# Two load queues, a full-width leftover pass, a third product buffer and new orders in a one-core FFT and MLP kernel

## The chip, the cores and the metric

The kernel runs on 1 core of one Trainium2 chip. The metric is the device time of one execution in microseconds (us), as the median of several runs. A profiled execution gives the trace that the text reads; its engines are called PE (matmul), PEld (weight load), DVE, ACT, POOL and SP, as in the profile.

## The reference

```python
def reference(A_x, A_w_r, A_w_i, B_x, B_w_gate, B_w_up, B_w_down):
    x = A_x                                   # (1, 2048, 576) bf16
    h = x + A(layernorm(x), A_w_r, A_w_i)     # A: rfft2 over both axes, times (w_r + i w_i), irfft2
    return h + B(layernorm(h), B_w_gate, B_w_up, B_w_down)
    # B(x) = (gelu(x @ w_gate) * (x @ w_up)) @ w_down, F = 4608
```

A is a two-dimensional real Fourier transform of the 2048 x 576 input, a product with a given spectrum and the transform back. B is a gated MLP. Each has a layer norm ahead of it, without scale and shift, and a residual.

## The kernel before

Everything is written engine by engine: a small class `Prog` records operations with the tiles that they read and write, puts each on the engine named, in the order in which it is recorded, and places the semaphore waits. Nothing is scheduled at run time. The order comes from three strings of short words that loops read: `SEQ1` (the front: first layer norm and first transform step), `SEQF` (the spectral middle) and `SEQ` (transform back, second layer norm, start of the MLP). A word is a letter for an operation and a number; a last letter A, D or P names the engine (ACT, DVE, POOL). Since each engine runs in order, a word's place counts only against the words of the same engine, and whatever waits holds up all that is behind it on its engine.

*Loads.* `LORD` lists the pieces of x (tile XO, 16 row tiles of 128 x 576) and of the cos/sin table (ATB, 16 tiles of 128 x 128) in order of issue; "x4-8" is tiles 4 to 7 of x. All are issued by SP, followed there by the other tables (FT, BT, VT, DT, ...) and the spectrum (WS).

*The front* (`SEQ1`). The 16 tiles form six groups, (0,2), (2,4), (4,7), (7,10), (10,13), (13,16). Three tiles (3, 4 and 13) get their statistics on ACT, a sum (`S`, L471) and a sum of squares (`Q`, L475); the others on DVE by two half-width `bn_stats` each (`B`, L480). Then for each group: `v` the variance (L486, L488, L491), `q` the square root on ACT (L495), `c` the reciprocal on DVE (L500), `x` the scaled table ATS = ATB times the reciprocal deviation (POOL L505, or DVE L510), `n` the negated right half of x into XN (POOL L552), `M` the matmuls (L536), `E` the copy of their result from PSUM into U (L547, on ACT or DVE). For the last groups `E` copies the first half of U's columns and `F` the second. `k` stands for dummy matmuls on a zero tile ZD (L521): k14 is 14 of them at the start, k104 four for group 1's bank, k202 two for group 2's.

In `M` five passes k = 0 to 4 go over the columns of x. Passes 0 to 3 add or subtract 128-column pieces of the left and right half. Pass 4 takes the leftover columns 256 to 287 and 544 to 575, as two matmuls with 32 output rows each:

```python
parts = [(XO[:, c, 256 + 288 * h:288 + 288 * h], 32 * h, 32 * h + 32, True, True) for h in range(2)]
```

so pass 4 fills 64 of 128 partitions of U, and POOL zeroes the others first (L466). PSUM has 8 banks and a group uses five in turn, so a group's matmuls also wait for older evictions.

*The middle* (`SEQF`), for 16 column groups: `D` six matmuls with FT on U (L606) and an ACT copy to CUS; `B` four matmuls with BT (L616) and an ACT copy to YS (L598); `T` products of YS with the spectrum into TP (DVE L625); `Z` sums of TP into ZS and ZR (DVE L636, L639); `V` four matmuls with VT (L646) and an ACT copy to V; `R` two matmuls for the last 32 columns (L658) and a masked copy into VR on DVE (L661); `w` the negated imaginary spectrum (DVE L630). TP, CUS and YS rotate through 2, 3 and 2 buffers.

*The start of the second half* (`SEQ`): `I` and `N` transform back (L731, L774), the residual add (L791) and the second layer norm for six row tiles (`s`, `q`, `c`, `n`, `e`), `z`, `D`, `A` transpose a normalised tile through PE (L836), and `g`, `h` are the first MLP matmuls. After that come the MLP's four blocks of gate/up matmuls (L872) and down matmuls (L973), with the other ten row tiles worked in between.

Of the kernel before, what the change touches and what calls it, by code (L numbers as in the profile page):

```python
# [4 lines left out]
BF16 = mybir.dt.bfloat16  # L5
F32 = mybir.dt.float32
ACTF = mybir.ActivationFunctionType
ALU = mybir.AluOpType

S, D, K2 = 2048, 576, 289  # L10
KW = 288
HK = 144
NZ = 5
# [10 lines left out]
SEQ1 = """k14 Q3 B1 B0 n0 S3 n2 v0 B2 v1 q0 q1 c0 x0D M0 S4 c1 Q4 B5 B6 E4A E2A v2 B7 q2 n1 E0A E1A x1P c2 k104 M1 B8 x2P B9 E6A n3 v3 E3A E5A E8A q3 k202 M2 B10 B12 E9A n4 E11A E12A S13 c3 B11 E10A E7A v4 x3P M3 B14 q4 c4 E13A E14A x4P B15 Q13 v5 E17A q5 E16A E15D M4 c5 E19A E20A x5D E18D E23A n5 E22D E21D E24A M5 E25A F23D F24A E26A F25D E27A E29A F29A E28D F28D F22A F26D F27A""".split()  # L24
LORD = "x0-2 x2-4 a0-4 x4-8 a4-8 x8-12 x12-16 a8-16".split()
SPLIT = tuple(int(w[1:-1]) for w in SEQ1 if w[0] == "F")
ACT_TILES = tuple(int(w[1:]) for w in SEQ1 if w[0] == "Q")
SEQF = """w0 w1 D0 D1 D2 B0 T0 D3 B1 Z0 T1 B2 D4 T2 D5 Z1 B3 B4 T3 D6 Z2 w2 D7 Z3 B5 V1 V0 T4 T5 Z4 B6 w3 B7 T6 D8 Z5 T7 V2 D9 Z6 B8 T8 V3 Z7 V4 D10 B9 R0 D11 V5 Z8 B10 T9 R1 T10 B11 D12 Z9 V6 D13 Z10 B12 T11 D14 T12 B13 V8 Z11 V7 B14 T13 Z12 D15 Z13 T14 V9 R2 V10 Z14 B15 V13 T15a T15b V11 Z15a V12 Z15b R3 V14 V15 R4""".split()
VENG = [('act',), ('act',), ('act',), ('act',), ('act',), ('act',), ('act',), ('act',), ('act',), ('act',), ('act',), ('act',), ('act',), ('act',), ('act',), ('act', 'act')]
DENG, BENG = ['act', 'act', 'act', 'act', 'act', 'act', 'act', 'act', 'act', 'act', 'act', 'act', 'act', 'act', 'act', 'act'], ['act', 'act', 'act', 'act', 'act', 'act', 'act', 'act', 'act', 'act', 'act', 'act', 'act', 'act', 'act', 'act']  # L30
SEQ = """I0 I1 N0 I2 s0 N1 I3 S1 q0 N2 I4 c0 e0 s2 q1 n0 n1 N3 I5 c1 z0 n2 s3 e1 D1 N4 N5 e2 q2 c2 n3 e3 D2 g10 g00 h10 z3 h00 g20 g01 h20 h01 g21 g11 h21 h11""".split()
# [14 lines left out]
def build_tables():  # L46
# [36 lines left out]
    def ang(d, k):  # L83
        return np.pi * (((2 * d[:, None] + 1) * k[None, :]) % (2 * D)) / D

    fr = np.zeros((6, 128, 2, HK))
    dr = np.concatenate([np.arange(256, 288), np.arange(544, 576)])
    for o, kk in enumerate((k2o, k2e)):
        for h, fn in enumerate((np.cos, np.sin)):
            for t in range(2):  # L90
                fr[3 * o + t, :, h] = fn(ang(np.arange(128 * t, 128 * t + 128), kk))
            fr[3 * o + 2, 0:64, h] = fn(ang(dr, kk))
# [220 lines left out]
def _build(nc, A_x, A_w_r, A_w_i, B_w_gate, B_w_up, B_w_down, out):  # L313
# [28 lines left out]
    XN = sb.alloc("XN", [128, NT, 288], BF16)  # L342
# [49 lines left out]
    TP = sb.alloc("TP", [128, 2, 2, 2, KW], BF16)  # L392
# [15 lines left out]
    def bank(b, p0=0, p1=128, c0=0, c1=512):  # L408
        return PS[p0:p1, b * 512 + c0:b * 512 + c1]
# [15 lines left out]
    def x_load(i, c0, c1):  # L425
        P.dma(SP, XO[:, c0:c1, 0:D], xv[:, c0:c1, :], f"x{i}", w=[("X", c) for c in range(c0, c1)])

    def atb_load(i, c0, c1):
        P.dma(SP, ATB[:, c0:c1, :], tabs[:, c0:c1, :], f"atb{i}", w=[("ATB", c) for c in range(c0, c1)])

    for i, w in enumerate(LORD):
        (x_load if w[0] == "x" else atb_load)(i, int(w[1:].split("-")[0]), int(w.split("-")[1]))
# [33 lines left out]
    P.op(POOL, lambda g: g.memset(U[64:128, 4, :, :, :], 0.0), w=["Uz"])  # L466
# [11 lines left out]
    def ln1_tile(c):  # L478
        for h in range(2):
            P.op(DVE, lambda v, c=c, h=h: v.bn_stats(ST1[:, c, h, :], XO[:, c, 288 * h:288 * h + 288]), r=[("X", c)], w=[("ST1", c, h)])  # L480

    def ln1_var(i):
        c0, c1 = GROUPS[i]
        for c in range(c0, c1):
            if c in ACT_TILES:
                P.op(DVE, lambda v, c=c: v.tensor_scalar(TM[:, 0, c:c + 1], SA[:, 0, c:c + 1], SA[:, 0, c:c + 1], 1.0 / (D * D), op0=ALU.mult, op1=ALU.mult), r=[("SA0", c)], w=[("TM", c)])  # L486
            else:
                P.op(DVE, lambda v, c=c: v.bn_aggr(MV1[:, c, :], ST1[:, c, :, :]), r=[("ST1", c, 0), ("ST1", c, 1)], w=[("MV1", c)])  # L488
        for c in range(c0, c1):
            if c in ACT_TILES:  # L490
                P.op(DVE, lambda v, c=c: v.tensor_scalar(MV1[:, c, 1:2], SA[:, 1, c:c + 1], 1.0 / D, TM[:, 0, c:c + 1], op0=ALU.mult, op1=ALU.subtract), r=[("SA1", c), ("TM", c)], w=[("MV1", c)])  # L491
# [23 lines left out]
    def a_bank(i, k):  # L515
        return (5 * i + AORD.index(k) + ABASE) % 8
# [6 lines left out]
    def a_mm(i):  # L523
        c0, c1 = GROUPS[i]
        for k in AORD:
            b = a_bank(i, k)
            for c in range(c0, c1):
                o = 128 * (c - c0)
                if k == 4:
                    parts = [(XO[:, c, 256 + 288 * h:288 + 288 * h], 32 * h, 32 * h + 32, True, True) for h in range(2)]  # L530
                else:
                    d0 = 128 * (k // 2)
                    x2 = XN[:, c, d0:d0 + 128] if k % 2 else XO[:, c, 288 + d0:416 + d0]
                    parts = [(XO[:, c, d0:d0 + 128], 0, 128, True, False), (x2, 0, 128, False, True)]
                for lhs, p0, p1, s, e in parts:
                    P.op(PE, lambda t, b=b, lhs=lhs, p0=p0, p1=p1, s=s, e=e, o=o, c=c: t.matmul(bank(b, p0, p1, o, o + 128), lhs, ATS[:, c, :], start=s, stop=e),  # L536
                         r=[("X", c), ("ATS", c)] + ([("XN", c)] if k % 2 else []), w=[("PS", b)])

    def a_ev(n, eng, late=False):
        i, k = n // 5, AORD[n % 5]  # L540
        hs = (1,) if late else (0,) if n in SPLIT else (0, 1)
        g0, g1 = 8 * hs[0], 8 * hs[-1] + 8
        c0, c1 = GROUPS[i]
        m, b, w = c1 - c0, a_bank(i, k), 64 if k == 4 else 128
        src = bank(b, 0, w, 0, 128 * m).rearrange("p (n g e) -> p n g e", n=m, g=16)[:, :, g0:g1, :]
        dst = U[0:w, k, g0:g1, c0:c1, :].rearrange("p g n e -> p n g e")
        fn = (lambda v: v.tensor_copy(dst, src)) if eng == DVE else (lambda a: a.activation(dst, src, ACTF.Copy))  # L547
        P.op(eng, fn, r=[("PS", b)] + ([("EV", n)] if late else []), w=[("U", i, k, h) for h in hs] + ([] if late else [("EV", n)]))

    def x_neg(i):  # L550
        c0, c1 = GROUPS[i]
        P.op(POOL, lambda g: g.tensor_scalar(XN[:, c0:c1, :], XO[:, c0:c1, 288:D], -1.0, 1.0, op0=ALU.mult, op1=ALU.mult),  # L552
             r=[("X", c) for c in range(c0, c1)], w=[("XN", c) for c in range(c0, c1)])

    ENG = {"A": ACT, "D": DVE, "P": POOL}
    RUN1 = {"k": idle_mm, "S": act_sum, "Q": act_sq, "B": ln1_tile, "v": ln1_var, "q": ln1_sqrt, "c": ln1_rs, "M": a_mm, "x": ln1_scale, "E": a_ev, "F": lambda n, eng: a_ev(n, eng, True), "n": x_neg}
    P.op(ACT, lambda a: a.activation(SA[:, 0, 0:1], EPT[:, 0:1], ACTF.Sqrt), r=["EPT"], w=[("SA0", 0)])
# [14 lines left out]
    P.alias([("XN", c) for c in range(NT)], [("V", g, c) for g in range(NG) for c in range(2)])  # L572
    uk = [[("U", i, k, h) for i in range(len(GROUPS)) for h in range(2)] + (["Uz"] if k == 4 else []) for k in range(5)]
# [27 lines left out]
    def st_D(i, eng=ACT):  # L601
        b0, s3 = FB["D", i], i % 3
        for o in range(2):
            b = b0 + o
            for m, us in enumerate((1 - o, 3 - o, 4) if o == 0 else (4, 1 - o, 3 - o)):
                P.op(PE, lambda t, b=b, m=m, us=us, o=o: t.matmul(bank(b, 0, 128, 0, 2 * HK), U[:, us, i, :, :], FT[:, 3 * o + (2 if us == 4 else us // 2), :], start=(m == 0), stop=(m == 2)),  # L606
                    r=[("U", q, us, i // 8) for q in range(len(GROUPS))] + (["Uz"] if us == 4 else []) + ["FT"], w=[("PS", b)])
        ev(eng, CUS[:, s3, :, :].rearrange("p a (j r) -> p a j r", r=2), banks(b0, 2, 2 * HK).rearrange("p r (a j) -> p a j r", a=2),
           [("PS", b0), ("PS", b0 + 1)], [("CU", s3)])
# [10 lines left out]
    def st_T(i, q0=0, q1=KW, hs=(0, 1)):  # L620
        g, sl = GORD[i], i % 2
        w3 = WS[:, 1, g, 1 + q0:1 + q1]
        w4 = bass.AP(w3.tensor, w3.offset, [list(w3.ap[0]), [NG * K2, 2], [-NG * K2, 2], [1, q1 - q0]])
        y4 = YS[:, sl, :, q0:q1].unsqueeze(1).to_broadcast([128, 2, 2, q1 - q0])
        P.op(DVE, lambda v: v.tensor_tensor(TP[:, sl, :, :, q0:q1], y4, w4, op=ALU.mult),  # L625
             r=[("Y", sl), ("Wn", i)] + (wkeys[0] if 1 <= g < 9 else wkeys[1] if g else wkeys[0] + wkeys[1]), w=[("T", sl, h) for h in hs])
# [6 lines left out]
    def st_Z(i, hs=(0, 1)):  # L633
        sl, z3 = i % 2, i % NZ
# [291 lines left out]
    P.alias([("ATB", c) for c in range(NT)], [("AT", f) for f in gu_early])  # L926
# [14 lines left out]
    fdead += [("T", a, h) for a in range(2) for h in range(2)] + [("Z", a) for a in range(NZ)] + [("ZR", a, h) for a in range(2) for h in range(4)]  # L941
# [102 lines left out]
```

## Time and profile before

| | us |
|---|---|
| median of 3 runs (lowest, highest) | 491.55 (491.47, 491.59) |
| profiled execution | 491.75 |
| its span, first to last instruction | 490.0 |
| PE busy in the span | 482.7 |
| first matmul of M0 | 7.29 |
| first matmul of stage D | 20.22 |
| first matmul of I0 | 48.66 |
| first MLP matmul (L872) | 57.40 |

The span is that of the slowest, here the only, core. Busy time of PE is the time in which at least one matmul is under way, with modelled ends. A row of a group of instructions gives busy time, the mean of one, and the idle time of its engine just before them with what ended it. The granted TensorE clock is 1.000 for the core. Idle time of an engine matters only where the chain of waits passes through it.

### The profile page before, as it was taken

To read this page: it belongs to the slowest core of one execution; us is meant where nothing else is said; L and a number is where in the kernel's file an instruction comes from. 1 tells how busy PE (TensorE), PEld (TensorE's weight loads), DVE (VectorE), ACT (ScalarE), POOL (GpSimd) and SP (SyncE) were. 2 spreads that over 40 slices of the span, in tenths; PEclk is the share of its full clock that TensorE was granted. 3 is DMA by queue.
4 is the path that set the end of the run, shared out by engine and by line. 5 is a ranking of instruction groups with operands and counts; after the bars stand their busy time and mean duration, and the time that the engine had idled before them with its cause. 6 is when DMAs were issued, how large, how long until landed. Compare 5 with 4: busy or idle time off the path is not lost.

```text
span 490.0 us, 9967 instructions
## 1 busy us (share of the span) xinstructions
PE 482.7 (99%) x4391; PEld 311.6 (64%) x4392; DVE 193.6 (40%) x397; ACT 151.2 (31%) x297; POOL 31.8 (6%) x58
## 2 busy tenths in 40 slices
PE   7999999999999999999999999999999999999998
PEld 3787788888888744444577644444677544444775
DVE  6799733433576634333311144433211233333111
ACT  6999743223322222322200033233100122323000
POOL 6411441000000020000000000000000000000000
DMA  8990999100001071100000001000000000000000
GB/s 284 248 313 6 354 363 351 30 15 2 1 16 37 18 233 23 26 1 1 2 18 16 17 18 23 17 1 0 7 19 19 7 1 0 1 2 1 13 20 18
DMA packets 25148, 31.20 MB, mean 64 GB/s; under 512 B 11440, under 2 KB 17840, under 8 KB 25104
## 3 DMA queue, kind: packets, MB, share of 16 engines
q1 hardware_dynamic: 22208, 18.62, 13.1%
q0 software_dynamic: 2896, 11.95, 7.0%
q8 instruction: 34, 0.56, 0.5%
q14 instruction: 10, 0.08, 0.1%
HBM read 26.22 MB, written 2.36 MB: 58 GB/s over the span
## 4 chain that ended last, share of the span: by engine, by line
PE 94%; DVE 2%; DMA 1%; issue 1%; POOL 0%; ACT 0%; SPq 0%; DVEq 0%; POOLq 0%
PE PS L872 57%; PE PS L973 29%; PE PS L606 2%; PE PS L536 2%; DMA XO<-in_A_x_dram 1%; PE PS L890 1%; PE PS L616 1%; PE PS L731 1%; DVE TP L625 1%; PE PS L774 1%; PE PS L646 1%; PE PS L908 1%; DVE VR L661 0%; DVE ZS L636 0%; POOL XN L552 0%
## 5 line engine op out<-in xcount | busy, mean ns | idle before, releaser
L872 PE MATMUL PS<-HT,WG 64*128 64x512 bf16 (+1 forms) x2160 | 229.0, 371 | 0.1
L872 PEld LDWEIGHTS PS<-HT,WG 64*128 64x128 bf16 x2160 | 130.3, 94 | 96.9 <-issue 1.1
L881 DVE TENSOR_TENSOR AT<-GL,PS 128x512 bf16<-128x512 bf16 (+1 forms) x147 | 99.3, 676 | 178.3 <-ACT GL L880 178.3
L880 ACT ACTIVATE GL<-PS 128x512 bf16<-128x512 f32 (+1 forms) x147 | 86.5, 588 | 262.9 <-PE PS L872 251.6
L973 PE MATMUL PS<-WD,AT 128*128 128x288 bf16 (+2 forms) x1152 | 144.9, 286 | 0.0
L973 PEld LDWEIGHTS PS<-WD,AT 128*128 128x128 bf16 x1152 | 110.7, 98 | 30.6 <-ACT GL L880 0.8
L872 PE MATMUL PS<-HT,WGX 64*128 64x512 bf16 x486 | 53.4, 376 | 0.0
L976 DVE TENSOR_TENSOR OS<-PS,XO 128x288 bf16<-128x288 f32 (+2 forms) x32 | 14.6, 456 | 94.5 <-PE PS L973 94.4
L872 PEld LDWEIGHTS PS<-HT,WGX 64*128 64x128 bf16 x486 | 23.7, 94 | 28.8
L606 PE MATMUL PS<-FT,U 128*128 128x288 bf16 x96 | 13.7, 286 | 0.0
L625 DVE TENSOR_TENSOR TP<-YS,WS 128x1152 bf16<-128x1152 bf16 (+2 forms) x17 | 11.9, 719 | 2.9 <-ACT YS L598 2.6
L536 PE MATMUL PS<-ATS,XO 128*128 128x128 bf16 (+1 forms) x128 | 10.1, 221 | 2.9 <-ACT U L547 1.2
L895 ACT ACTIVATE EB<-PS 128x288 f32<-128x288 f32 x10 | 4.1, 411 | 27.7 <-PE PS L890 27.7
L480 DVE BATCH_NORM_STATS2 ST<-XO 128x6 f32<-128x288 bf16 x26 | 10.0, 438 | 3.9 <-DMA XO<-in_A_x_dram 3.9
L536 PEld LDWEIGHTS PS<-ATS,XO 128*128 128x128 bf16 (+1 forms) x128 | 7.5, 97 | 5.5 <-DVE ATS L510 1.5
L606 PEld LDWEIGHTS PS<-FT,U 128*128 128x128 bf16 x96 | 9.3, 98 | 2.3
L913 DVE TENSOR_TENSOR XO<-PS,XO 128x576 bf16<-128x576 f32 x10 | 7.6, 757 | 8.0 <-PE PS L908 8.0
L598 ACT ACTIVATE CUS<-PS 128x576 bf16<-128x576 f32 x16 | 10.4, 655 | 0.5 <-PE PS L606 0.2
L598 ACT ACTIVATE YS<-PS 128x576 bf16<-128x576 f32 x16 | 10.1, 655 | 0.0
L547 ACT ACTIVATE U<-PS 128x256 bf16<-128x256 f32 (+5 forms) x29 | 9.7, 391 | 1.0 <-PE PS L536 0.8
L616 PE MATMUL PS<-CUS,BT 128*128 128x288 bf16 x64 | 10.0, 286 | 0.0
L901 DVE TENSOR_TENSOR QB<-PS,EB 128x288 f32<-128x288 f32 x20 | 8.2, 452 | 3.3 <-ACT EB L895 3.3
(79 smaller groups left out, 207.5 us busy)
## 6 DMA issues: line engine op xcount, KB each, us to landing
WD<-in_B_w_down_dram POOLq DMA_DIRECT2D x9, 576.0 KB, 12.2
WG<-in_B_w_up_dram SPq DMA_DIRECT2D x4, 1152.0 KB, 7.5
WG<-in_B_w_gate_dram POOLq DMA_DIRECT2D x4, 1152.0 KB, 9.9
out_dram<-OS SPq DMA_DIRECT2D x30, 72.0 KB, 1.6
XO<-in_A_x_dram SPq DMA_DIRECT2D x3, 576.0 KB, 7.2
WGX<-in_B_w_up_dram SPq DMA_DIRECT2D x1, 1152.0 KB, 6.1
WGX<-in_B_w_gate_dram POOLq DMA_DIRECT2D x1, 1152.0 KB, 9.9
HT<-HN SPq DMA_TRANSPOSE x60, 2.4
```

The lines of the kernel that those rows point to most:

```text
L480: P.op(DVE, lambda v, c=c, h=h: v.bn_stats(ST1[:, c, h, :], XO[:, c, 288 * h:288 * h + 288]), r=[("X", c)], w=[("ST1", c, h)])
L536: P.op(PE, lambda t, b=b, lhs=lhs, p0=p0, p1=p1, s=s, e=e, o=o, c=c: t.matmul(bank(b, p0, p1, o, o + 128), lhs, ATS[:, c, :], start=s, sto ...
L547: fn = (lambda v: v.tensor_copy(dst, src)) if eng == DVE else (lambda a: a.activation(dst, src, ACTF.Copy))
L598: fn = (lambda v: v.tensor_copy(dst, src)) if eng == DVE else (lambda a: a.activation(dst, src, ACTF.Copy))
L606: P.op(PE, lambda t, b=b, m=m, us=us, o=o: t.matmul(bank(b, 0, 128, 0, 2 * HK), U[:, us, i, :, :], FT[:, 3 * o + (2 if us == 4 else us // ...
L616: P.op(PE, lambda t, b=b, tb=tb, m=m, s3=s3, sp_=sp_: t.matmul(bank(b, 0, 128, 0, KW), BT[:, sp_, tb, :], CUS[:, s3, m, :], start=(m == 0) ...
L625: P.op(DVE, lambda v: v.tensor_tensor(TP[:, sl, :, :, q0:q1], y4, w4, op=ALU.mult), r=[("Y", sl), ("Wn", i)] + (wkeys[0] if 1 <= g < 9 els ...
L872: op = P.op(PE, lambda t, h0=h0, kt=kt, wt=wt, b=b, s=(not second and j == 0), e=(second and j == n - 1): t.matmul(bank(b, 0, 128, c0, c1) ...
L880: P.op(ACT, lambda a: a.activation(GL[:, s2, c0:c1], bank(b0, 0, 128, c0, c1), ACTF.Gelu_apprx_tanh), r=[("PS", b0)], w=[("GL", s2)])
L881: P.op(DVE, lambda v: v.tensor_tensor(AT[:, f, c0:c1], GL[:, s2, c0:c1], bank(b0 + 1, 0, 128, c0, c1), op=ALU.mult), r=[("GL", s2), ("PS", ...
L973: P.op(PE, lambda t, b=b, d0=d0, d1=d1, f=f, p=p: t.matmul(bank(b, 0, 128, 0, d1 - d0), AT[:, f, 128 * p:128 * p + 128], WD[:, f, d0:d1], ...
L976: P.op(DVE, lambda v, b=b, d0=d0, d1=d1, p=p, c=c: v.tensor_tensor(OS[:, p % 2, d0:d1], bank(b, 0, 128, 0, d1 - d0), XO[:, c, d0:d1], op=A ...
```

## The change

- *Loads.* The order becomes x0-2, x2-4, a0-4, x4-8, x12-16 on SP, and a4-8, x8-12, a8-16 on ACT (marked "@"). ACT issues its three behind its first table load and first square root. The first three pieces stay where they were. SP's later loads follow three issues sooner.
- *Leftover pass.* XN grows from 288 to 320 columns. A new POOL operation `t` (x_tail) copies columns 256 to 287 of x behind XN's negated ones, and pass 4 becomes one matmul a tile on XN's last 128 columns. Its lower 64 rows hold columns that other passes cover; FT is zero there, and the sign is in FT. U's pass 4 is evicted over 128 partitions, and the memset of U falls away.
- *Statistics.* The halves of `bn_stats` are separate words (`B` and `b`); the square of the mean for ACT's tiles is a word of its own (`m`), for tile 3 on DVE and for tiles 4 and 13 on POOL.
- *TP* has three buffers.
- *Orders.* `SEQ1`, `SEQF` and `SEQ` are new. Among others, k104 stands before M0, c2 (group 2's reciprocal) behind statistics of tiles 8, 9 and 12 on DVE, and on POOL n2, m4 before x1P and t2, t3, n3 before x2P. In `SEQ` one PSUM copy goes to DVE (`J3`), one sum of squares from DVE to ACT (`s1`), and two transposed tiles are evicted by ACT.

The diff, cut to its core:

```diff
-SEQ1 = """k14 Q3 B1 B0 n0 S3 n2 v0 B2 v1 q0 q1 c0 x0D M0 S4 c1 Q4 B5 B6 E4A E2A v2 B7 q2 n1 E0A E1A x1P c2 k104 M1 B8 x2P B9 E6A n3 v3 E3A E5A E8A q3 k202 M2 B10 B12 E9A n4 E11A E12A S13 c3 B11 E10A E7A v4 x3P M3 B14 q4 c4 E13A E14A x4P B15 Q13 v5 E17A q5 E16A E15D M4 c5 E19A E20A x5D E18D E23A n5 E22D E21D E24A M5 E25A F23D F24A E26A F25D E27A E29A F29A E28D F28D F22A F26D F27A""".split()
-LORD = "x0-2 x2-4 a0-4 x4-8 a4-8 x8-12 x12-16 a8-16".split()
+SEQ1 = """n1 B1 t0 b0 b1 S3 B0 v0 k14 t1 q0 m3D B2 b2 c0 k104 Q3 v1 x0D n0 M0 q1 c1 B6 S4 n2 b5 B5 m4P b6 E1A E0A x1P M1 E3A B8 b7 Q4 v2 E2A b9 q2 t2 t3 n3 b12 c2 x2P t4 E7A E8A B7 b8 B9 v3 Q13 b10 k202 b11 E9A S13 q3 c3 m13P B10 E5A x3P n4 B11 E4A E6A M2 B12 E11A E10A E12A v4 q4 B14 M3 E15A c4 b15 E14A x4P E13A b14 E16A t5 B15 v5 n5 E18A M4 q5 E17D E20A c5 x5D E22D E19A E24D F24D E21A M5 E23A F23D E25A F25A E27D E29D F29D E26A E28A F22A F28A F26A F27D""".split()
+LORD = "x0-2 x2-4 a0-4 x4-8 x12-16 a4-8@ x8-12@ a8-16@".split()
-SEQF = """w0 w1 D0 D1 D2 B0 T0 D3 B1 Z0 T1 B2 D4 T2 D5 Z1 B3 B4 T3 D6 Z2 w2 D7 Z3 B5 V1 V0 T4 T5 Z4 B6 w3 B7 T6 D8 Z5 T7 V2 D9 Z6 B8 T8 V3 Z7 V4 D10 B9 R0 D11 V5 Z8 B10 T9 R1 T10 B11 D12 Z9 V6 D13 Z10 B12 T11 D14 T12 B13 V8 Z11 V7 B14 T13 Z12 D15 Z13 T14 V9 R2 V10 Z14 B15 V13 T15a T15b V11 Z15a V12 Z15b R3 V14 V15 R4""".split()
+SEQF = """w0 D0 D1 D2 w1 B0 D3 B1 T0 T1 B2 T2 w2 B3 D4 Z1 D5 D6 B4 D7 Z0 T3 B5 Z2 D8 T4 Z3 T5 V0 R0 B6 D9 V1 Z5 B7 T6 w3 Z4 T7 B8 T8 V2 V3 Z7 D11 V5 B9 Z8 Z6 T9 D10 D12 R1 B10 D13 B11 T10 Z10 B12 V4 V7 D14 T11 B13 V6 Z9 T12 Z12 Z11 B14 T13 D15 T14 V8 Z13 V9 Z14 B15 R2 V13 V10 T15a T15b V14 V12 Z15a V11 Z15b R3 V15 R4""".split()
-SEQ = """I0 I1 N0 I2 s0 N1 I3 S1 q0 N2 I4 c0 e0 s2 q1 n0 n1 N3 I5 c1 z0 n2 s3 e1 D1 N4 N5 e2 q2 c2 n3 e3 D2 g10 g00 h10 z3 h00 g20 g01 h20 h01 g21 g11 h21 h11""".split()
+SEQ = """I0 I1 N0 I2 N1 J3 s0 N2 s1 q0 c0 n0 I4 s2 n1 N3 q1 c1 I5 e0 D0 e1 A1 e2 n2 N4 N5 s3 q2 c2 n3 D2 g00 g10 h00 e3 A3 h10 g20 g01 h20 h01 g11 g21 h11 h21""".split()
...
-            fr[3 * o + 2, 0:64, h] = fn(ang(dr, kk))
+            fr[3 * o + 2, 64:96, h] = -fn(ang(np.arange(544, 576), kk))
+            fr[3 * o + 2, 96:128, h] = fn(ang(np.arange(256, 288), kk))
...
-    XN = sb.alloc("XN", [128, NT, 288], BF16)
+    XN = sb.alloc("XN", [128, NT, 320], BF16)
...
-    TP = sb.alloc("TP", [128, 2, 2, 2, KW], BF16)
+    TP = sb.alloc("TP", [128, 3, 2, 2, KW], BF16)
...
+    P.op(ACT, lambda a: a.activation(SA[:, 0, 0:1], EPT[:, 0:1], ACTF.Sqrt), r=["EPT"], w=[("SA0", 0)])
     for i, w in enumerate(LORD):
-        (x_load if w[0] == "x" else atb_load)(i, int(w[1:].split("-")[0]), int(w.split("-")[1]))
+        c0, c1 = (int(v) for v in w[1:].rstrip("@").split("-"))
+        (x_load if w[0] == "x" else atb_load)(i, c0, c1, ACT if w[-1] == "@" else SP)
...
-    P.op(POOL, lambda g: g.memset(U[64:128, 4, :, :, :], 0.0), w=["Uz"])
...
+    def act_mean2(c, eng):
+        P.op(eng, lambda v: v.tensor_scalar(TM[:, 0, c:c + 1], SA[:, 0, c:c + 1], SA[:, 0, c:c + 1], 1.0 / (D * D), op0=ALU.mult, op1=ALU.mult), r=[("SA0", c)], w=[("TM", c)])
...
-                    parts = [(XO[:, c, 256 + 288 * h:288 + 288 * h], 32 * h, 32 * h + 32, True, True) for h in range(2)]
+                    parts = [(XN[:, c, 192:320], True, True)]
...
+    def x_tail(i):
+        c0, c1 = GROUPS[i]
+        P.op(POOL, lambda g: g.tensor_scalar(XN[:, c0:c1, 288:320], XO[:, c0:c1, 256:288], 1.0, 1.0, op0=ALU.mult, op1=ALU.mult),
+             r=[("X", c) for c in range(c0, c1)], w=[("XT", c) for c in range(c0, c1)])
...
     def st_T(i, q0=0, q1=KW, hs=(0, 1)):
-        g, sl = GORD[i], i % 2
+        g, sl, tl = GORD[i], i % 2, i % 3
```

## The prediction

> **What bounds the kernel now.** I read the page first, then a table of windows by stage, then the chain in order of time, then the timeline of each engine over the first 64 us, and last the DMA windows. The page says that TensorE is the kernel:
>
> ```profile
> PE 482.7 (99%) x4391; PEld 311.6 (64%) x4392; DVE 193.6 (40%) x397; ACT 151.2 (31%) x297; POOL 31.8 (6%) x58
> ```
>
> Only 7.3 of 490.0 us have no matmul. The windows (stretch, its length, then busy time of PE, PEld, DVE, ACT, POOL) show where:
>
> ```profile
> 7.29:10.30 3.01, 2.30 (x25) 1.32 (x25) 2.78 (x12) 2.58 (x9) 2.20 (x3) 1.00 0.99 377
> 10.30:15.04 4.74, 3.49 (x51) 2.71 (x52) 4.74 (x21) 4.23 (x14) 3.48 (x4) 1.00 1.08 329
> 15.04:20.40 5.36, 5.36 (x92) 4.71 (x93) 4.78 (x19) 4.90 (x16) 2.94 (x8) 1.00 1.10 255
> 20.40:35.80 15.40, 15.40 (x130) 12.47 (x129) 12.29 (x33) 15.14 (x30) 1.53 (x2) 1.00 0.96 305
> 35.80:48.60 12.80, 12.56 (x106) 9.95 (x104) 12.69 (x29) 12.46 (x24) 0.99 (x2) 1.00 0.05 8
> ```
>
> The reader is to see three things. From 63.9 us on the change touches nothing. From 20.4 to 48.6 PE, ACT and (in the second part) DVE are full together. And up to 15 us PE is not the limit: DVE is busy for all 4.74 us before 15.04 while PE idles for 1.25. The chain says what that stage hangs on (start, length, piece):
>
> ```profile
> 2.12 5.55 DMA XO<-in_A_x_dram
> ...
> 7.74 0.92 POOL XN L552
> ...
> 8.80 0.68 POOL XN L552
> ...
> 9.63 0.62 POOL ATS L505
> ...
> 12.82 0.86 ACT U L547 x2
> 13.69 0.66 ACT JNK L471 x2
> 14.35 0.65 ACT U L547 x2
> ...
> 15.04 5.33 PE PS L536 x90
> 20.38 2.21 PE PS L606 x18
> ```
>
> It waits for the x piece of tiles 4 to 7, which lands at 7.7; then POOL, ACT and DVE pass the work around. Stage D (L606) begins at 20.22 in the timeline. What the front does to that moment is what the change is worth, to first order.
>
> **Time base.** The profiled execution took 491.75 us, 1.75 beyond its span; the median of the runs is 491.55. I sum shifts against 491.75 and take 0.20 off for the median.
>
> **Part 1, the leftover pass.** L536 did two 32-row matmuls a tile for k = 4, now one of 128: 16 matmuls fewer. In the timeline matmuls of this stage start 0.056 us apart (12.01, 12.07, 12.12), so PE work falls by 16 x 0.056 = 0.9 us. But PE waits for the scaled tables in this stage; only the last group's share counts (27 instead of 30 matmuls, 0.17). The evictions go from 64 to 128 partitions at the same time (479 and 482 ns for 384 columns), and stage D keeps its six matmuls. The memset of U that falls away (1.81 us on POOL) lay before POOL's first x piece, so it frees nothing.
>
> **Part 2, more on POOL.** The six x_tail copies are not in the trace. XN of 576 elements costs 674 ns and of 864 costs 912, which is 0.83 ns an element plus 0.2: 0.25 for 64 and 0.28 for 96 elements. POOL starts an instruction some 0.15 after the one before (8.66 to 8.80), so they add 6 x 0.42 = 2.5 us, and two moved squares of the mean (0.2 each, like the NM rows) 0.7. Bounds per copy: 0.35 (the NM rows) to 0.83 (an XN of 576 with its gap). These are not hidden: POOL runs in order, and x1P, x2P, x3P, x4P and n5 stand behind them.
>
> **Part 3, the loads.** ScalarE gets a4-8, x8-12 and a8-16; it issues them at about 2.2, when its first square root ends (2.02 + 0.20), and was idle until 4.43, so issuing costs it nothing. What do two queues do to each other? Where POOL's and SyncE's weight loads overlap, the DMA windows give (packets, MB, share), for 59 to 61 us:
>
> ```profile
> q0 software_dynamic: 113, 0.52, 67.5%
> q1 hardware_dynamic: 113, 0.26, 36.4%
> ```
>
> The engines take packets in turn, one from each queue, and both together move 0.39 MB/us; SyncE's queue alone moved 0.40 to 0.42 from 9 to 12 us. So the second queue brings no bandwidth; it lets x8-12 and a4-8 go beside x4-8 instead of behind it. The Trainium skill (DMA: Bandwidth & Descriptors, section Issuing engines are not separate DMA queues) states the same, that DMAs of several issuers share 16 engines and interleave, which speaks against this change; the packet counts agree.
> SyncE's first bytes came 1.2 us after its first issue, so ScalarE's come at 3.4. By then some 210 of SyncE's 512 packets up to the end of x4-8 are done (168 by 3.2, 352 by 4.0). The other 300 are met by 300 of ScalarE's 384: a4-8, x8-12 and a third of a8-16, 0.81 MB, 2.0 us. Against it, SyncE's queue moved only 0.22 MB from 4.0 to 5.2, where 0.47 would fit; a second queue can fill that, 0.6 us. So x4-8 lands at 7.7 + 1.4 = 9.1 (bounds: 7.7, and 9.7 without the filling), x8-12 at about 8.8 (10.3 before), x12-16 at 11.2 as before.
>
> **Part 4, the chain after x4-8.** Durations are those of the rows: half statistics 0.385, aggregate 0.1, sqrt 0.2, ACT sum or square 0.68, XN 0.91, table scaling on POOL 0.83, each with POOL's 0.15.
> - M1: POOL does n2 (9.1 to 10.0), m4 (to 10.5), x1P (10.65 to 11.25). M1 at 11.3, before 10.30. M0 stays near 7.2.
> - M2: POOL goes on with t2, t3, n3 (to 13.1), then x2P. M2 at 14.1, before 11.96. DVE is ready earlier: four halves, two, v2, two, c2 at 12.7.
> - M3: DVE does five halves, v3, c3 at 15.0; x3P ends 15.9. M3 at 16.0, before 15.04.
> - M4: four more halves and v4, c4 at 16.9; x4P ends 18.0, before 16.6.
> - M5: three halves, v5, E17, c5 at 18.95, three table scalings (0.17 each); n5 ends at 19.4. M5 from 19.5 to 21.0.
> Stage D thus begins near 21.0 instead of 20.22: **+0.8**. ACT then has three evictions of 0.38 and eight halves of 0.25 to do from 18.9, so its first CUS eviction comes at 22.0, before 21.43: +0.6.
>
> **Part 5, stages D to R and the early second half.** Matmul work there is unchanged: 16 x 6 + 16 x 4 at 0.1225, 16 x 4 + 10 at 0.109, 27.7 us, in 28.44 from 20.22 to 48.66. So at most 0.77 us can be won, with 0.3 more up to 63.9. The third TP buffer removes no duration; DVE runs T and Z in order, so it only permits the new order. ACT needs 32 x 0.55 + 15 x 0.53 + 0.7 = 26.3 of its 27.4 us there, and it starts 0.6 late. The new order puts five V evictions behind the last YS, before four: 0.5 more of ACT at the end, while 0.65 of PE work is moved behind it too. I take 0 (bounds -0.8 and +1.0), and carry +0.7 in all.
>
> **The sum.** 491.75 + 0.7 = 492.45 profiled, **492.3** as a median; 0.2% (about 1.0 us, what a measurement of this kernel can tell from no change) leaves it just inside no change. Its own range is 491.6 to 493.0.
>
> **Rivals.**
> *Early pieces (0.30).* The second queue fills gaps without delaying x4-8 (7.7), and x12-16 lands near 10.2. The same chain then gives M2 at 12.6, M3 at 14.7, M4 at 16.8, M5 at 18.3 and D at 19.85: -0.4, or -0.9 if part 1 counts whole; with up to 0.77 of the middle's stalls gone, 489.9 to 491.3, centre 490.5. For it: the poor rate at 4.0 to 5.2. Against: 113 packets to 113.
> *The clock falls (0.15, slower).* M0 ends at 8.2 and, with the four dummies of k104 now ahead of it, PE stands idle until 11.3, 3.1 us; before, 1.2 was the longest. The first dummies started 0.427 apart and the later ones 0.2, so an idle PE runs at half rate. From a gap of about 3 us on, M2 would take 3.0 instead of 1.5, M3 start at 17.1, and D begin near 21.9 if PE recovers within the 3.4 us that the start took: 493.4 in all; if only at M5, 4 us more. Against: no gap in this trace shows it, and each granted clock is 1.00. The Trainium skill (TensorE: Matmul & The Clock Gate, section Part 1) gives an idle window of about 3.4 us before the rate halves; by that the gap just falls short.
> *The middle loses (0.15).* ACT's idle 1.1 us stays, and Z0 behind Z1 and five V's behind YS15 make I0 wait: +1.0 beyond the forecast, 493.2. For it: ACT and PE are both full there. Against: before, half the stalls sat at the same end.
>
> **Chances and range.** Forecast 0.40 (0.25 within the bound, 0.15 above), early pieces 0.30 (0.18 below, 0.12 within), clock 0.15 (above), middle 0.15 (0.13 above, 0.02 within). So faster 0.18, same 0.39, slower 0.43. The lowest tenth ends at 490.3, inside the early pieces; the highest begins at 494.0, inside the clock and the middle.
>
> **What would show it.** x4-8's landing near 9.1 and M1 near 11.3 prove part 3; XN, x_tail and ATS back to back on POOL from 9 to 14 prove part 2; M5 waiting for n5 and DVE's tables, with D at 21.0, proves part 4; from D to I0 some 28.4 us, part 5. L536 rows of 0.107 apart after 11 us mean the falling clock. x4-8 at 7.7 and D before 20 mean the first rival, and then I am wrong.

## The result

The changed kernel took 493.67 us (median of 6 runs, 493.14 to 494.85) beside 491.57 for the kernel before (6 runs): a ratio of 1.0044, interval 1.0034 to 1.0054, 2.1 us slower. The profiled execution took 493.92 with a span of 492.1.

The page of the changed kernel and the same stretches as before (length, busy time of PE, PEld, DVE, ACT, POOL, then the granted clock):

```profile
PE 482.3 (98%) x4376; PEld 286.5 (58%) x4376; DVE 193.1 (39%) x392; ACT 151.5 (31%) x298; POOL 31.9 (6%) x65
...
7.29:10.30 3.01, 1.18 (x18) 1.02 (x18) 2.39 (x11) 1.85 (x7) 1.78 (x5) 1.00 1.04 424
10.30:15.04 4.74, 3.14 (x27) 2.42 (x28) 4.70 (x19) 4.02 (x15) 3.78 (x8) 0.64 1.09 290
15.04:20.40 5.36, 4.29 (x74) 3.95 (x72) 4.16 (x18) 5.36 (x18) 4.01 (x6) 1.00 1.11 240
20.40:35.80 15.40, 15.40 (x148) 12.63 (x145) 12.94 (x35) 14.67 (x31) 2.76 (x9) 1.00 1.01 304
35.80:48.60 12.80, 12.80 (x111) 10.38 (x110) 12.42 (x31) 12.58 (x25) 0.00 (x0) 1.00 0.01 5
```

PE idles longer in each stretch up to 20.4, and in the second the clock is at 0.64 of full. The chain of the changed kernel:

```profile
2.12 7.55 DMA XO<-in_A_x_dram
...
9.69 1.55 DVE ST L480 x4
11.24 0.62 POOL ATS L506
...
11.90 1.69 PE PS L537 x14
...
15.78 1.96 ACT U L548 x6
17.74 0.19 ACT RS L496
...
17.96 0.19 DVE RS L501
...
18.22 0.84 POOL ATS L506
...
19.11 3.25 PE PS L537 x54
22.36 2.22 PE PS L611 x18
```

The same piece, x4-8, is awaited, but 7.55 us from its issue where it was 5.55. From the timelines, first matmuls in us:

| | before | changed | shift |
|---|---|---|---|
| M0 | 7.29 | 8.97 | +1.68 |
| M1 | 10.30 | 11.90 | +1.60 |
| stage D | 20.22 | 22.19 | +1.97 |
| I0 | 48.66 | 50.55 | +1.89 |
| first MLP matmul | 57.40 | 59.16 | +1.76 |

At stage D the kernel is 1.97 us behind. Up to the end of the last matmul 0.5 of that is won back (489.03 beside 487.59, +1.44), and behind it 0.7 more is lost: the span goes on for 3.1 us there, before for 2.4. The last pieces of the two chains, before and then changed, show where ("issue" is time in which the engine waits for nothing that the profile shows):

```profile
487.64 0.04 issue
487.69 0.29 DVE OS L976
```

```profile
489.08 0.41 issue
489.49 0.29 DVE OS L981
```

The last copy on DVE starts 0.36 later behind its matmul, and the rest of the 0.7 falls on the last store behind it. What happens ahead of stage D begins with the loads. ACT's timeline in the changed kernel (start, length):

```profile
0.72 1.28 ACT L431 ACT_TABLE_LOAD   x1 [0.72 <-PEq L1034]
0.86 0.35 ACTq L223 DMA_DIRECT2D ATB<-c_atab  x1
1.25 0.47 ACTq L223 DMA_DIRECT2D XO<-in_A_x_dram  x1
1.75 0.45 ACTq L223 DMA_DIRECT2D ATB<-c_atab  x1
2.02 0.20 ACT L431 ACTIVATE SA<-EPT 128x1 f32<-128x1 f32 x1
6.61 0.68 ACT L472 ACTIVATE JNK<-XO 128x576 bf16<-128x576 bf16 x1 [4.38 <-DMA XO<-in_A_x_dram]
```

ACT's queue issues the three loads while the table load is still running, from 0.86, 0.13 behind SyncE's first. The DMA window from 2.5 to 4 us (packets, MB, share) has them in turn:

```profile
q1 hardware_dynamic: 133, 0.27, 61.3%
q10 hardware_dynamic: 138, 0.13, 27.7%
```

and so the front is not unchanged in time: x0-2 lands at 4.3 (3.7 before), x2-4 at 6.6 (4.4; ACT's first sum waits for it in the line above), a0-4 at 8.1 (4.8).

### The profile page after: what moved, and what is told of

Same layout as the page of the kernel before. It is cut to its first block, busy times and chain, and to the rows that moved or that the text cites. A ratio compares the mean times of both kernels' runs of the same rounds, so it can differ in the third digit from the quotient of the medians.

```text
span 492.1 us, 9930 instructions
## 1 busy us (share of the span) xinstructions
PE 482.3 (98%) x4376; PEld 286.5 (58%) x4376; DVE 193.1 (39%) x392; ACT 151.5 (31%) x298; POOL 31.9 (6%) x65
## 4 chain that ended last, share of the span: by engine, by line
PE 96%; DMA 2%; ACT 1%; DVE 1%; POOL 0%; SPq 0%; issue 0%; DVEq 0%
PE PS L877 57%; PE PS L978 29%; PE PS L611 2%; PE PS L621 2%; DMA XO<-in_A_x_dram 2%; PE PS L651 1%; PE PS L895 1%; PE PS L537 1%; PE PS L736 1%; PE PS L779 1%; ACT U L548 1%; PE PS L913 0%; DVE ST L480 0%; PE PS L841 0%; POOL ATS L506 0%; SPq L223 0%
## 5 line engine op out<-in xcount | busy, mean ns | idle before, releaser
L877 PEld LDWEIGHTS PS<-HT,WG 64*128 64x128 bf16 x2160 | 104.6, 94 | 122.2 <-issue 0.7
L981 DVE TENSOR_TENSOR OS<-PS,XO 128x288 bf16<-128x288 f32 (+2 forms) x32 | 14.6, 457 | 94.8 <-PE PS L978 94.8
L537 PE MATMUL PS<-ATS,XO 128*128 128x128 bf16 x96 | 9.4, 231 | 4.0 <-DVE ATS L511 2.0
L630 DVE TENSOR_TENSOR TP<-YS,WS 128x1152 bf16<-128x1152 bf16 (+2 forms) x17 | 11.9, 720 | 2.6 <-ACT YS L603 2.1
L537 PEld LDWEIGHTS PS<-ATS,XO 128*128 128x128 bf16 x96 | 7.3, 104 | 5.6 <-POOL ATS L506 3.0
L603 ACT ACTIVATE CUS<-PS 128x576 bf16<-128x576 f32 x16 | 10.3, 657 | 0.6
L548 ACT ACTIVATE U<-PS 128x384 bf16<-128x384 f32 (+2 forms) x29 | 9.8, 440 | 0.7 <-PE PS L537 0.7
## 6 DMA issues: line engine op xcount, KB each, us to landing
WD<-in_B_w_down_dram POOLq DMA_DIRECT2D x9, 576.0 KB, 11.9
```

The lines of the kernel that those rows point to most:

```text
L537: P.op(PE, lambda t, b=b, lhs=lhs, s=s, e=e, o=o, c=c: t.matmul(bank(b, 0, 128, o, o + 128), lhs, ATS[:, c, :], start=s, stop=e), r=[("X", ...
L630: P.op(DVE, lambda v: v.tensor_tensor(TP[:, tl, :, :, q0:q1], y4, w4, op=ALU.mult), r=[("Y", sl), ("Wn", i)] + (wkeys[0] if 1 <= g < 9 els ...
L877: op = P.op(PE, lambda t, h0=h0, kt=kt, wt=wt, b=b, s=(not second and j == 0), e=(second and j == n - 1): t.matmul(bank(b, 0, 128, c0, c1) ...
L981: P.op(DVE, lambda v, b=b, d0=d0, d1=d1, p=p, c=c: v.tensor_tensor(OS[:, p % 2, d0:d1], bank(b, 0, 128, 0, d1 - d0), XO[:, c, d0:d1], op=A ...
```

## The experiments

The kernel before was measured again with each of three groups of runs, at 491.58, 491.57 and 491.63; each ratio is against the time of its own group. Theory 1: taking turns from 0.86 on delays the pieces that set the front. Its rivals: the new orders and POOL's copies; the clock; the middle.

**One queue.** The changed kernel with the old list of loads.

```diff
-LORD = "x0-2 x2-4 a0-4 x4-8 x12-16 a4-8@ x8-12@ a8-16@".split()
+LORD = "x0-2 x2-4 a0-4 x4-8 a4-8 x8-12 x12-16 a8-16".split()
```

> The changed kernel with the list of loads of before, all on SyncE; everything else as changed. Theory 1 (the second queue takes turns with the first from the start and delays x2-4, a0-4 and x4-8, which set the front): x2-4 lands near 4.4 and x4-8 near 7.7 again, M0 starts near 7.2, stage D near 20.5, and the time is 491.6 to 492.1 us, 1.6 to 2.0 under the changed kernel. Rival (the copies on POOL and the new orders cost it, whatever the landing): stage D stays at 21.5 or later, the time at 493.0 or more.

492.31, ratio 1.0015 (1.0006 to 1.0024); stage D at 20.58. That is above the forecast of theory 1 (492.1 at most) and below the rival's. So 1.36 of the 2.1 us go with the second queue, but not all: 0.7 stay. In the profiled run they stay at the end of the kernel: its last matmul ends at 487.66, as before (487.59), and the span goes on for 3.0 us behind it. In the front, x4-8 landed at 8.1 here (7.7 before), and M0 came at 8.10, not 7.2, although its table was ready at 7.1: the four dummies now ahead of it ran until then. On DVE the new order has words that wait for x8-12, which lands at 10.4:

```profile
8.15 1.54 DVE L480 BATCH_NORM_STATS2 ST<-XO 128x6 f32<-128x288 bf16 x4 [0.85 <-DMA XO<-in_A_x_dram]
10.43 0.82 DVE L480 BATCH_NORM_STATS2 ST<-XO 128x6 f32<-128x288 bf16 x2 [0.74 <-DMA XO<-in_A_x_dram]
```

**Issue at 2.2.** ScalarE's loads made to wait for its first square root, which is what the prediction had assumed.

```diff
-... f"ld{i}", w=[("X", c) ...
+... f"ld{i}", r=[("SA0", 0)] if eng == ACT else [], w=[("X", c) ...   # the same for ATB
```

> The changed kernel, but ScalarE's three loads wait for its own first square root, so that they are issued from 2.2 us as the prediction had assumed, not at 0.86. Theory 1, with the prediction's own chain: M0 near 7.2 to 7.6, x4-8 near 9.1, M1 near 11.3, stage D near 21.0, the time 492.3 to 492.6. If it is the sharing at any time that counts and not the early start: x4-8 near 9.7 again and 493.2 or more. If the second queue does no harm once the first pieces are in: x4-8 near 7.7 and 491.6 or less.

493.98, ratio 1.0050 (1.0037 to 1.0063), no better. Up to M1 the prediction's chain comes out: x4-8 at 8.85 (9.1 forecast), M0 at 6.87 (7.2 to 7.6), M1 at 11.07 (11.3). Then it fails, at 22.03 for stage D instead of 21.0, since x8-12 lands at 11.9 and not at 8.8. DVE's timeline of this run:

```profile
8.85 1.54 DVE L480 BATCH_NORM_STATS2 ST<-XO 128x6 f32<-128x288 bf16 x4 [1.68 <-DMA XO<-in_A_x_dram]
11.88 0.82 DVE L480 BATCH_NORM_STATS2 ST<-XO 128x6 f32<-128x288 bf16 x2 [1.49 <-DMA XO<-in_A_x_dram]
```

ScalarE's queue, issued at 2.25, moved 4 packets from 4 to 5 us and 27 from 5 to 6; only from 6 on were the two even (71 to 67, 58 to 55, 50 to 53). A later start spares the first pieces and delays x8-12 instead, which the new order wants first. The granted clock fell in this run too (0.51 from 11.0 to 14.5), and its share of the 22.03 is not measured apart.

**Dummies in the gaps**, two runs on the clock.

```diff
-... k104 Q3 v1 x0D ... x1P M1 ...
+... k112 Q3 v1 x0D ... x1P k108 M1 ...      # e3; in e7: k107 and k106
```

> The changed kernel with 8 more dummy matmuls ahead of M0 and 8 ahead of M1, which fill most of the two gaps of 2.0 and 1.8 us. Clock theory (the half rate from 11.2 to 14.7 us holds up the evictions of M1 and with them square root and reciprocal of group 3): the granted clock stays at 1.00, M1 takes 1.0 instead of 2.0, M3 to M5 come up to 0.7 earlier, the time is 492.9 to 493.3. Rival (M2 waits for its table until 14.6 anyway, so the half rate is hidden): the time stays at 493.6 to 493.8.

493.63, ratio 1.0039 (1.0027 to 1.0052). The clock stayed at 1.00 from 10.3 to 15, but the dummies themselves held M0 up to 9.47, when its table had been ready since 8.50, and M1 to 12.20 (11.75), so the run does not decide. With fewer:

> The changed kernel with 3 more dummies ahead of M0 and 6 ahead of M1, fewer than the 8 and 8 of the run before, which had held M0 and M1 up themselves. Clock theory: the granted clock stays at 1.00, M1 starts with its table at 11.9 and takes 1.0 instead of 2.0, its evictions and the square root of group 3 come 0.4 to 0.7 earlier, stage D at 21.5 to 21.8, the time 493.0 to 493.4. Rival: 493.5 to 493.8 again.

493.38, ratio 1.0037 (1.0025 to 1.0050). M1 is ready at 12.02 and at full rate, stage D starts at 21.63 where the changed kernel had 22.19. The windows of the changed kernel, then of this run:

```profile
8.97:11.20 2.23, 1.18 (x18) 0.99 (x18) 1.74 (x7) 1.55 (x7) 1.17 (x2) 0.99 1.00 408
11.20:14.60 3.40, 2.70 (x20) 2.05 (x20) 3.40 (x17) 2.68 (x10) 2.87 (x5) 0.50 1.13 271
```

```profile
10.30:15.04 4.74, 3.02 (x30) 1.74 (x30) 4.74 (x19) 4.58 (x17) 3.83 (x8) 1.00 1.11 281
```

The half rate (0.50 from 11.2 to 14.6) cost 0.3 us by the medians, 0.56 by stage D; the intervals overlap, so its size stands no closer than that. The executions of the changed kernel say the same: five of six had a mean granted clock of 0.993 to 0.997 and took 493.36 to 494.85, the one with 1.000 took 493.14. In the run with one queue the two executions below 0.999 were the two slowest (493.28 and 493.43, median 492.31).

**The new middle alone**, on the kernel before.

```diff
+SEQF, SEQ and the three TP buffers of the changed kernel; loads, leftover pass, SEQ1 as before
```

> The kernel before with the third product buffer and the new orders of the middle and of the start of the second half alone; loads, leftover pass and front as before. As forecast: from stage D to I0 28.3 to 28.5 us as before, the time within 0.2 us of before. Rival (the new middle repairs stalls or makes new ones): 0.5 us or more off, either way.

491.25, ratio 0.9994 (0.9985 to 1.0003): no change that can be told. Stage D to I0 takes 28.35 us (28.44 before, 28.36 in the changed kernel), I0 to the MLP 8.60 (8.74).

**Two queues alone**, on the kernel before.

```diff
+LORD, x_load, atb_load and the early square root of the changed kernel; all else as before
```

> The kernel before with only the list of loads and the two queues of the changed kernel (ScalarE issues from 0.86); old orders, old leftover pass, old middle. If the queue alone carries the loss: x2-4 lands near 6.6 and x4-8 near 9.7 as in the changed kernel, M0 near 9.0, stage D near 21.6 to 22.2, the time 493.0 to 493.7. If the new orders are needed for the loss (the old ones absorb late pieces): 492.3 or less.

493.34, ratio 1.0038 (1.0025 to 1.0051), with x4-8 at 9.6, M1 at 12.22, stage D at 22.14, and the granted clock at 1.00. The earlier pieces were less late than forecast: x2-4 landed at 5.4 and not 6.6, M0 came at 8.34 and not 9.0. One edit loses 1.77 us with the old orders, by way of x4-8: theory 1 is shown.

**The tables alone on the second queue.**

```diff
+LORD = "x0-2 x2-4 a0-4 x4-8 x8-12 x12-16 a4-8@ a8-16@".split()   # on the run above
```

> The kernel before, but with only the two table pieces a4-8 and a8-16 (0.39 MB in 256 packets) on ScalarE's queue from 0.86, and all of x on SyncE; the run with x8-12 on it too (0.98 MB) took 493.34. If it is the bytes that go between SyncE's packets: less than half the delay, x4-8 near 8.4, the time 492.1 to 492.5. If it is the number of packets or the mere second queue: x4-8 near 9.3 and 493.0 or more. If the gap that SyncE's queue alone leaves at 4.4 to 5.2 takes them up: x4-8 at 7.7 and 491.4 to 491.8.

491.83, ratio 1.0005 (0.9996 to 1.0013). M0 comes 0.7 later (7.99) as x0-2 lands at 4.4, but x4-8 lands at 7.9, and stage D at 20.43 is 0.2 later. That is nearest to the third reading, that the gap of SyncE's queue takes the tables up (x4-8 at 7.7, 491.8 at most), and below the reading by bytes (492.1 to 492.5). With 256 instead of 384 packets almost nothing is lost, so it is neither the second queue as such nor the count of packets. Between this run and the one with two queues alone only x8-12 changes its queue, and with its 0.59 MB on ScalarE's the kernel takes 1.5 us longer; whether by its bytes, its larger packets or its place was not split.

**The leftover pass alone**, on the kernel before.

```diff
-n0 S3 n2 v0 ... q2 n1 E0A E1A x1P c2 ... n3 v3 ... x3P M3 ... n5 E22D
+n0 t0 S3 n1 t1 n2 v0 ... q2 E0A E1A x1P t2 c2 ... n3 t3 v3 ... x3P t4 M3 ... n5 t5 E22D
+the matmul, FT, U and XN of the changed kernel
```

> The kernel before with only the full-width leftover pass; the six copies stand on POOL where its rows showed room (t0, n1 and t1 ahead of n2). By the prediction's part 1 the last groups on PE give 0.2 to 0.5 us: stage D at 19.8 to 20.2, the time 491.1 to 491.6. Rival (the copies on POOL cost more than the matmuls give): stage D at 20.5 or later, 491.9 or more.

490.86, ratio 0.9987 (0.9978 to 0.9996), faster by 0.7. The chain:

```profile
14.84 4.68 PE PS L535 x81
19.52 2.21 PE PS L610 x18
```

M3 to M5 are 81 matmuls without a break where before had 90 in 5.33 us: 0.65 us. Stage D begins at 19.36, 0.86 earlier; the other 0.2 is M3's start, in a run in which x4-8 landed 0.2 earlier than before (7.5). No POOL row is in the chain: the copies stood in POOL's idle time.

**One queue, order mended.**

```diff
-E3A B8 b7 Q4 v2 E2A b9 q2 t2 t3 n3 b12 c2 x2P t4 E7A
+E3A Q4 v2 E2A b7 q2 t2 c2 x2P B8 b9 t3 n3 b12 t4 E7A      # on the run with one queue
```

> As the run with one queue (492.3), but with group 2's variance, square root, reciprocal and table (v2, q2, c2, x2P) ahead of the statistics of tiles 8, 9 and 12 and of the copies for tiles 7 to 9, which wait for x8-12 and x12-16. If these words in front of c2 and x2P were its 0.7 us: M2 near 11.9 instead of 13.4, stage D at 20.0 to 20.3 instead of 20.6, the time 491.5 to 491.9. If ACT or POOL is full anyway: no change, 492.2 to 492.4.

491.99, ratio 1.0014 (1.0005 to 1.0023). M2 starts at 11.82 instead of 13.43, but stage D at 20.37, only 0.2 earlier: M2's last passes now wait 1.85 us for an eviction on ACT. The medians differ by 0.3, but the intervals overlap, and x4-8 landed 0.4 earlier here than in the run with one queue, so it stays open whether the words in front of c2 cost anything. The last matmul ends at 487.22, 0.4 earlier than before; what keeps this run above before is the end of the kernel, 3.0 us behind the last matmul.

**The changed kernel with the old front order.**

```diff
-SEQ1 of the changed kernel
+SEQ1 of the run with the leftover pass alone; two queues, leftover pass, new middle as changed
```

> The changed kernel with the front order of before (with the copies for the leftover pass put in as in the run with that alone); two queues, leftover pass, new middle as changed. By the sum of the parts (two queues +1.77, leftover pass -0.71, middle -0.33): 492.3, so the new front order costs some 1.3 of the changed kernel's 2.1. If the new front order suits the two queues: 493.5 or more.

492.57, ratio 1.0021 (1.0012 to 1.0030), stage D at 21.43. The new front order costs 1.1 us (493.67 less 492.57), and with one queue 1.5 (492.31 of the run with one queue, less the 490.79 of the next run, which differ in little else). Some 0.7 of either lies behind the last matmul: from there to the end of the span it is 2.9 to 3.2 us in all six kernels with the new front order, as it stands or mended, and 2.3 to 2.4 in the seven with the old. In the last 2.2 us of these six, and of no other, a packet of an instruction queue (q14) moves; why the front order brings that about is not shown. In the front itself, stage D of this run is at 21.43 beside 21.63 in the run with fitted dummies, so with two queues little more than the clock's 0.3 is left there.

**Leftover pass and new middle**, on the kernel before.

```diff
+the two runs "leftover pass alone" and "new middle alone" in one kernel; old loads, old front order
```

> The kernel before with the full-width leftover pass (as in the run with that alone, 490.86) and the new middle and second half with the third product buffer (alone 491.25); old loads, old front order. If the parts add: stage D near 19.4, I0 near 47.7, the time 490.4 to 490.7, below both kernels. If the earlier stage D only moves the wait to ACT in the middle: 490.8 or more.

490.79, ratio 0.9980 (0.9971 to 0.9988): below both kernels, and no better than the leftover pass alone can be told to be. Its x4-8 landed at 7.9 in the profiled run and its stage D began at 19.81.

The parts, then: two queues +1.8, leftover pass -0.7, new middle -0.3 (not told from zero) give 492.3, and the kernel with just these took 492.57; the new front order adds 1.1 to reach 493.67, of which some 0.7 comes at the end of the kernel and some 0.3 from the clock.

## Why the prediction was right or wrong

The direction was right and 493.67 lies in the range, but the likeliest number, 492.3, is 1.4 too low: 493.67 is above its own range of 491.6 to 493.0. That it lies in the whole range is in part luck. The part above 493.0 was there mainly for the clock and the middle; the middle lost nothing, the clock 0.3 to 0.6, and 0.7 came from the end of the kernel, which no rival held. Point by point:

- *Part 3, the loads.* That the queues take packets in turn, and that this speaks against the change, is shown. The step that failed is "it issues them at about 2.2, when its first square root ends": the loads went out at 0.86, beside the table load (that ACT issues them behind its first table load and square root, as the change was described, is wrong as well). The price was therefore put on x4-8 alone (+1.4, measured +2.0), while x2-4 (+2.2), a0-4 and with them M0 (+1.7) were held to be untouched. The issue time alone was not the miss, since the run that issued at 2.25 took 493.98.
- *Part 3, x8-12.* With the issue at 2.2 its landing would have been wrong too: "at about 8.8" against 11.9 measured, as the second queue, issued at 2.25, began to move at about 4.7 and not 1.2 us behind its issue. (SyncE's own first packets came at 1.7 to 1.8, 1.0 us behind its first issue, where the prediction read 1.2.) In the changed kernel it landed at 7.3.
- *Part 4, the chain.* The rows held, and given the landing of x4-8 (0.6 later than forecast) the chain came out up to M2: 14.68 beside 14.1 and 0.6. In the run with fitted dummies, where x4-8 was 0.7 late and the clock held, it came out to its end: M2, M4 and stage D at 14.79, 18.56 and 21.63, beside 14.1, 18.0 and 21.0 and 0.7 each. The further 0.6 at stage D of the changed kernel is the clock, which the sum did not hold. But +0.8 at stage D mixes the late x4-8 and the order; the prediction took the old order as the yardstick only through the moments of M1 to M5 and never priced the two changes by themselves.
- *Part 1, the leftover pass.* Mis-sized: "only the last group's share counts", 0.17, where with the old order the whole of M3 to M5 counts, 0.65 in the rows; 0.7 measured. With this the loss of the rest was 2.8 and not 2.1.
- *Part 2, POOL's copies.* Right in size: 0.24 for 64 and 0.27 for 96 elements (0.25 and 0.28). That they are "not hidden" depends on the place: alone, put in POOL's idle time, they were.
- *Part 5, the middle.* Right: 28.36 us from stage D to I0, 28.4 forecast.
- *From 63.9 us on.* "The change touches nothing" there is wrong: 0.7 us is lost behind the last matmul, a term that the sum did not have.
- *Rivals.* Early pieces: refuted by the landings. The clock: it did fall, but cost 0.3 us by the medians, 0.56 at stage D, and not 1.7, because M2 waited for its table until 14.6 in any case and the rate was back by then (with the clock at 1.00 M2 began at 14.79). The trigger differed from the one weighed: no gap was longer than 2.0 us, but between 6.9 and 11.2 PE had only M0's 1.2 us of work. The Trainium skill (TensorE: Matmul & The Clock Gate, section Part 1) gives an idle window of about 3.4 us; this trace shows the fall without one. The middle: did not lose.

## What to carry to other kernels

In these runs a second load queue was not behind the first but beside it (133 packets to 138): what it carried was paid for by what the first was carrying at the time. 0.39 MB that nobody waited for early cost 0.2 us, not told from zero, 0.98 MB cost 1.8. A place behind other work in program order did not say when the queue issues (0.86, not 2.2); look for the issuing row in the trace. Compare the ends of the two traces as well as the stage that was changed: here 0.7 us lay behind the last matmul. And measure the parts of a bundle by themselves: one part (0.7 us faster) was buried under two that lost 2.8.

## What had not been expected of the hardware

- ACT's queue issued three loads from 0.86 to 2.2 us while its table load ran from 0.72 to 2.00.
- ScalarE's queue needed 1.6 to 2.1 us from its first issue at 0.86 to its first packets (between 2.4 and 3.0 in six profiled runs), and 2.4 when issued at 2.25 (4.6 to 4.8); SyncE's needed 1.0 in the kernel before (0.73 to 1.7 or 1.8).
- The granted clock fell to 0.50 at 11.2 us after 1.2 us of matmuls in the 4.3 us before, and was back at 14.6. In the run with two queues alone, with gaps of 2.3 and 1.6 us, it stayed at 1.00.
- The landing of x4-8 moved between 7.5 and 8.2 us over six profiled runs whose loads are those of before, and that of x2-4 between 5.4 and 6.7 over five with the loads of the changed kernel.
- With the new front order the end of the kernel, behind its last matmul, was some 0.7 us longer in six of six traces; the cause stays open.
